# An attention and mixture kernel on one core: the first two pairs by TensorE instead of transfers, and the second expert product's first half in slices of 128 columns

## The chip, the cores and the metric

The kernel runs on one core of a Trainium2 chip. The metric is device time in microseconds (us), from the start to the end of one execution. The core has TensorE (matrix products, written to PSUM in 8 banks), DVE (VectorE), ACT (ScalarE), GpSimd (POOL) and SyncE (SP), which only issues transfers here. Transfers run on 16 DMA engines. The engines work through their own queues in program order and wait for one another by semaphores.

## The reference

Attention with a decay bias, then a soft mixture of experts over its output:

```python
cum = np.cumsum(np.maximum(s, 0.0), axis=-1)
bias = -(cum[:, :, :, None] - cum[:, :, None, :])
scores = np.where(causal, -1e9, scale * q @ k.T + np.minimum(bias, 0.0))
attn = softmax(scores) @ v                     # 8 batches x 8 heads, 576 x 64
logits = x @ phi                               # x: 4608 x 512, 32 slots
slot_input = softmax(logits, axis 0).T @ x     # 8 experts x 4 slots
slot_out[e] = np.maximum(slot_input[e] @ w1[e], 0.0) @ w2[e]
out = softmax(logits, axis 1) @ slot_out       # 4608 x 512
```

All arrays are fp32. Each expert has w1 of 512 x 1024 and w2 of 1024 x 512.

## The kernel before

**Pairs.** The 64 heads are worked on in 32 pairs of heads; a pair's q and k lie transposed on 128 partitions, 64 for each head. For pair p the steps are these. `load.p` fetches q and k, `cast.p.i` (ACT, line 341) rounds q (i=0) or k (i=1) to the matmul's short form fp32r, and `low.p.i` (DVE, line 347) subtracts that from the original to keep the low part. `mx.p.g` (TensorE, lines 375 to 379) are four groups of products for the row maxima: q times k, plus ones times the running sums of s. `red.p.g.a` (DVE, lines 381 to 392) reduces them. `f0` (GpSimd, lines 403 and 404) splits the maxima in a high and a low part, `f1` (line 411) turns them by one TensorE transpose, `f2` (ACT, line 417) copies them out of PSUM, and `md` (lines 422 to 427) sends them by a transfer into rows of the tile `g`, four rows out of 128 spread to every 32nd partition and the next one. `cum.p` (lines 355 to 360) sends the running sums' high and low parts into `g` as well. `s.p.g` (lines 438 to 446) are the scores: three short-form products of high and low parts and one of `g`, which adds sums and maxima. `ex` (ACT) is the exponential, `cut` (GpSimd) sets what is above the diagonal to zero, `z` (GpSimd) and `sm` (TensorE) add up the rows, `ax` and `a` (TensorE, lines 522 and 533) multiply by v in full fp32. fp32 products show as two instructions each, fp32r products as one.

**Sums.** Ahead of the pairs `s` is loaded to 64 partitions (line 238), clamped (DVE, line 267), summed by a scan (line 268), and split into `cumhl`, high (line 271) and low (line 272), both on DVE. The pairs 0 to 3 take their sums from `cumhl`; `cw` (line 875) copies it to DRAM for the others.

**Order.** The whole program is written out in one order, the string ORDER, made by a planner; each engine and the SP queue take their steps in that order. A step `busy.n` is n fp32 products of the identity that nothing uses (line 937): filler for TensorE. Of the 46 in the head, 28 stand ahead of the first maxima, 9 behind mx.1.0, and 3 and 6 on either side of mx.2.0 and mx.1.2. SP, which issues most transfers, waits in its queue for whatever the next transfer needs: `load.p` needs the low parts of pair p-2, since there are two buffers.

**The end.** After the last pair come the mixture's products: `mlp1` (line 995), `turn` (line 1012), then `mlp2(half, eg)` (lines 1017 to 1030), for each half of 256 of the 512 output columns and each group of four experts 8 steps; `steps(m, n)` runs n of them. `pick(half)` (line 1035) adds up the experts' rows, and `part(b, n, half)` (lines 1055 to 1067) makes the outputs of n batches for that half by four row tiles of 32 partitions, copies them out on ACT and DVE and sends them, 512 rows a batch of 1 KB each. `heads` (line 1070) sends the first 64 rows of each batch. In the kernel before, the first half's products are finished, then the second half's steps are interleaved with the first half's parts. Weights are fetched up to the second product, through the same SP queue as the outputs.

Of the kernel before, what the change touches and what calls it, by code (L numbers as in the profile page):

```python
# [24 lines left out]
load.0 load.1 cast.0.1 cast.0.0 cast.1.1 low.0.1 cum.0 cast.1.0 low.0.0 cum.1 low.1.1 low.1.0 load.3 busy.28 mx.0.0  # L25
mx.0.1 cum.2 red.0.0.1 mx.0.2 red.0.0.0 load.2 red.0.1.1 mx.0.3 red.0.1.0 red.0.2.0 mx.1.0 red.0.3.0 red.0.3.1
red.0.2.1 red.1.0.1 busy.9 mx.1.1 f0.0 red.1.0.0 cast.2.0 mx.1.3 red.1.1.0 f1.0 red.1.1.1 f2.0 cast.2.1 red.1.3.0 md.0
busy.3 mx.2.0 low.2.0 mx.1.2 red.1.3.1 load_v.0 red.2.0.0 red.1.2.1 cw red.2.0.1 busy.6 s.0.0 red.1.2.0 s.0.2 f0.1
ex.0.0.1 ex.0.0.0 s.0.1 ex.0.2.1 cut.0.0 s.0.3 ex.0.2.0 ex.0.1.0 cut.0.2 mx.2.3 ex.0.1.1 zc.0 f1.1 red.2.3.0 a.0.0
f2.1 z.0.0 ex.0.3.0 md.1 red.2.3.1 cast.3.1 ax.0 a.0.1 ex.0.3.1 evx.0 load_v.1 mx.2.2 cut.0.3 mx.2.1 cut.0.1 red.2.2.0  # L30
z.0.1 cum.3 a.0.2 a.0.3 red.2.2.1 a.0.4 s.1.0 ev.0 z.0.2 red.2.1.1 cast.3.0 red.2.1.0 s.1.2 ex.1.0.0 z.0.3 low.3.1
f0.2 ex.1.0.1 s.1.1 ex.1.2.0 low.2.1 mx.3.0 ex.1.1.0 sm.0 red.3.0.1 load.4 cut.1.0 ex.1.2.1 red.3.0.0 load_v.2 f1.2
ex.1.1.1 cut.1.2 s.1.3 zc.1 f2.2 z.1.0 mx.3.3 md.2 ex.1.3.1 mx.3.2 ex.1.3.0 red.3.3.1 a.1.0 red.3.3.0 cum.4 cut.1.1
a.1.1 red.3.2.0 cut.1.3 z.1.1 cast.4.1 ax.1 a.1.2 red.3.2.1 cast.4.0 a.1.3 a.1.4 evx.1 low.3.0 mx.3.1 z.1.2 s.2.0
red.3.1.1 load.5 red.3.1.0 s.2.2 ex.2.0.1 z.1.3 ex.2.0.0 f0.3 s.2.1 ex.2.2.0 mx.4.0 ex.2.2.1 cut.2.0 f1.3 ex.2.1.0
red.4.0.0 sm.1 f2.3 low.4.0 ex.2.1.1 md.3 mx.4.3 zc.2 cut.2.1 red.4.0.1 ev.1 cut.2.2 mx.4.2 red.4.3.1 z.2.0 s.2.3
red.4.3.0 a.2.0 ex.2.3.1 cum.5 red.4.2.0 ex.2.3.0 cast.5.1 pre.0 a.2.1 cut.2.3 load_v.3 low.4.1 z.2.1 a.2.2 red.4.2.1
a.2.3 ax.2 a.2.4 evx.2 mx.4.1 load_v.4 ev.2 s.3.0 z.2.2 red.4.1.0 cast.5.0 red.4.1.1 cst s.3.2 low.5.0 z.2.3 ex.3.0.0
load.6 ex.3.0.1 s.3.1 ex.3.2.0 f0.4 mx.5.0 ex.3.1.0 sm.2 cut.3.0 red.5.0.0 ex.3.2.1 red.5.0.1 f1.4 ex.3.1.1 cut.3.2
low.5.1 s.3.3 zc.3 f2.4 z.3.0 mx.5.3 md.4 ex.3.3.1 mx.5.2 ex.3.3.0 red.5.3.0 mx.5.1 red.5.2.0 a.3.0 pre.1 load.7  # L40
cut.3.3 cum.6 red.5.3.1 a.3.1 cut.3.1 z.3.1 pre.2 red.5.1.1 a.3.2 red.5.2.1 ax.3 a.3.3 evx.3 cast.6.0 a.3.4 z.3.2
red.5.1.0 s.4.0 load_v.5 ev.3 low.6.0 f0.5 cast.6.1 s.4.2 ex.4.0.1 low.6.1 ex.4.0.0 s.4.1 z.3.3 ex.4.2.0 pre.3 cut.4.0
mx.6.0 ex.4.2.1 load.8 sm.3 red.6.0.0 ex.4.1.0 cut.4.2 phi ex.4.1.1 f1.5 e1.0.0.0 s.4.3 f2.5 cut.4.1 zc.4 md.5
red.6.0.1 mx.6.3 z.4.0 ex.4.3.0 mx.6.2 ex.4.3.1 red.6.3.0 cast.7.1 mx.6.1 cum.7 red.6.3.1 cast.7.0 ax.4 a.4.0 rw.0.0
evx.4 cut.4.3 red.6.2.0 z.4.1 a.4.1 red.6.2.1 a.4.2 pre.4 a.4.3 red.6.1.0 z.4.2 a.4.4 red.6.1.1 s.5.0 ev.4 load_v.6
low.7.0 f0.6 s.5.2 low.7.1 rd.0 ex.5.0.0 ex.5.0.1 s.5.1 z.4.3 ex.5.2.0 cut.5.0 rd.1 mx.7.0 ex.5.2.1 sm.4 ex.5.1.0
red.7.0.0 cut.5.2 ex.5.1.1 red.7.0.1 f1.6 load.9 s.5.3 f2.6 cut.5.1 zc.5 md.6 mx.7.3 z.5.0 ex.5.3.0 mx.7.2 ex.5.3.1
cast.8.1 mx.7.1 cum.8 cast.8.0 a.5.0 nr.0 cut.5.3 a.5.1 red.7.3.0 rd.2 z.5.1 a.5.2 red.7.3.1 a.5.3 nr.1 a.5.4 z.5.2
red.7.2.0 pre.5 s.6.0 rd.3 red.7.2.1 z.5.3 nat.0 ex.6.0.0 red.7.1.0 nat.1 natd.0 red.7.1.1 sm.5 natd.1 low.8.0 f0.7
ex.6.0.1 s.6.2 nr.2 low.8.1 s.6.1 cut.6.0 ex.6.2.0 ex.6.2.1 load.10 mx.8.0 ex.6.1.0 f1.7 nat.2 red.8.0.0 cut.6.2  # L50
ex.6.1.1 red.8.0.1 natd.2 s.6.3 cut.6.1 nr.3 f2.7 zc.6 mx.8.3 md.7 ex.6.3.0 z.6.0 mx.8.2 ex.6.3.1 red.8.3.0 cast.9.1
mx.8.1 red.8.3.1 cum.9 cast.9.0 lt.0 lt.1 red.8.2.0 pre.6 lt.2 cut.6.3 lt.3 z.6.1 red.8.2.1 nat.3 c0.0 c1.0 natd.3
red.8.1.0 nat0.0 red.8.1.1 z.6.2 ax.5 natd0.0 s0.0 s.7.0 load_v.7 evx.5 f0.8 ev.5 low.9.0 s1.0 s.7.2 ex.7.0.0 z.6.3
s2.0 ex.7.0.1 s.7.1 t2.0 s2p.0 ex.7.2.0 cut.7.0 mx.9.0 ex.7.2.1 sm.6 ex.7.1.0 red.9.0.0 cut.7.2 ex.7.1.1 red.9.0.1
f1.8 low.9.1 s.7.3 f2.8 cut.7.1 zc.7 md.8 t3.0 mx.9.3 z.7.0 mx.9.2 red.9.3.0 ex.7.3.0 cum.10 ex.7.3.1 t5.0 cast.10.1
red.9.3.1 mx.9.1 load.11 cast.10.0 a.6.0 red.9.2.0 cut.7.3 t6.0 z.7.1 a.6.1 red.9.2.1 a.6.2 red.9.1.0 z.7.2 a.6.3
red.9.1.1 a.6.4 ax.6 low.10.0 ax.7 evx.6 load_v.8 f0.9 s.8.0 evx.7 ev.6 t4.0 low.10.1 s.8.2 pre.7 ex.8.0.0 z.7.3
load.12 ex.8.0.1 s.8.1 ex.8.2.0 cut.8.0 mx.10.0 ex.8.2.1 sm.7 ex.8.1.0 red.10.0.0 cut.8.2 ex.8.1.1 t7.0 e1.1.0.0 zc.8
cut.8.1 z.8.0 red.10.0.1 rw.1.0 f1.9 t8.0 s.8.3 f2.9 md.9 mx.10.3 ex.8.3.0 mx.10.2 ex.8.3.1 red.10.3.0 cast.11.1
cut.8.3 mx.10.1 cum.11 red.10.3.1 cast.11.0 z.8.1 a.7.0 rd.4 red.10.2.0 a.7.1 rd.5 z.8.2 red.10.2.1 a.7.2 a.7.3  # L60
red.10.1.0 z.8.3 a.7.4 ax.8 red.10.1.1 ev.7 load_v.9 s.9.0 low.11.0 evx.8 f0.10 s.9.2 low.11.1 pre.8 ex.9.0.0 ex.9.0.1
s.9.1 load.13 nr.4 ex.9.2.0 cut.9.0 mx.11.0 ex.9.2.1 rd.6 sm.8 ex.9.1.0 red.11.0.0 cut.9.2 ex.9.1.1 red.11.0.1 f1.10
nat.4 nr.5 f2.10 cut.9.1 zc.9 md.10 s.9.3 natd.4 z.9.0 mx.11.3 ex.9.3.0 mx.11.2 ex.9.3.1 rd.7 red.11.3.0 cast.12.1
mx.11.1 red.11.3.1 cast.12.0 nat.5 cut.9.3 cum.12 red.11.2.0 a.8.0 natd.5 z.9.1 a.8.1 red.11.2.1 pre.9 a.8.2 z.9.2
red.11.1.0 a.8.3 red.11.1.1 a.8.4 z.9.3 low.12.0 ev.8 load_v.10 s.10.0 f0.11 nr.6 s.10.2 ex.10.0.0 ex.10.0.1 s.10.1
nr.7 ex.10.2.0 cut.10.0 low.12.1 mx.12.0 ex.10.2.1 lt.4 ex.10.1.0 red.12.0.0 cut.10.2 load.14 lt.5 ex.10.1.1
red.12.0.1 lt.6 cut.10.1 lt.7 sm.9 c0.1 f1.11 t2.1 c1.1 zc.10 nat.6 f2.11 s0.1 z.10.0 md.11 nat.7 natd.6 nat0.1 natd.7
s.10.3 s1.1 natd0.1 s2.1 mx.12.3 ex.10.3.0 cum.13 mx.12.2 ex.10.3.1 s2p.1 red.12.3.0 cast.13.1 pre.10 mx.12.1 cut.10.3
red.12.3.1 cast.13.0 a.9.0 z.10.1 t3.1 red.12.2.0 a.9.1 red.12.2.1 z.10.2 a.9.2 a.9.3 red.12.1.0 a.9.4 z.10.3 ax.9
ax.10 red.12.1.1 evx.9 load_v.11 s.11.0 evx.10 ev.9 low.13.0 f0.12 t4.1 s.11.2 low.13.1 ex.11.0.0 ex.11.0.1 s.11.1  # L70
load.15 ex.11.2.0 cut.11.0 mx.13.0 ex.11.2.1 sm.10 ex.11.1.0 red.13.0.0 cut.11.2 ex.11.1.1 red.13.0.1 f1.12 t5.1 f2.12
cut.11.1 zc.11 s.11.3 md.12 t6.1 z.11.0 mx.13.3 ex.11.3.0 mx.13.2 ex.11.3.1 red.13.3.0 cum.14 cast.14.1 mx.13.1
red.13.3.1 cast.14.0 a.10.0 pre.11 cut.11.3 red.13.2.0 z.11.1 a.10.1 red.13.2.1 a.10.2 a.10.3 z.11.2 red.13.1.0 a.10.4
ax.11 red.13.1.1 ev.10 load_v.12 s.12.0 low.14.0 z.11.3 evx.11 s.12.2 low.14.1 ex.12.0.0 f0.13 ex.12.0.1 s.12.1
ex.12.2.0 load.16 mx.14.0 ex.12.2.1 cut.12.0 sm.11 ex.12.1.0 red.14.0.0 ex.12.1.1 t7.1 cut.12.2 e1.2.0.0 zc.12
cut.12.1 z.12.0 red.14.0.1 rw.2.0 f1.13 t8.1 s.12.3 f2.13 md.13 mx.14.3 ex.12.3.0 mx.14.2 ex.12.3.1 red.14.3.0
cast.15.1 cut.12.3 mx.14.1 cum.15 red.14.3.1 cast.15.0 z.12.1 a.11.0 rd.8 red.14.2.0 a.11.1 rd.9 z.12.2 red.14.2.1
a.11.2 a.11.3 red.14.1.0 z.12.3 a.11.4 ax.12 pre.12 red.14.1.1 ev.11 s.13.0 load_v.13 low.15.0 evx.12 f0.14 s.13.2
low.15.1 ex.13.0.0 ex.13.0.1 s.13.1 load.17 nr.8 ex.13.2.0 cut.13.0 mx.15.0 ex.13.2.1 rd.10 sm.12 ex.13.1.0 red.15.0.0
# [1101 lines left out]
```

## Time and profile before

| what | us |
|---|---|
| median of 3 runs | 415.88 |
| lowest and highest | 414.98 and 417.01 |
| the profiled execution's own time | 415.59 |
| its span, first to last instruction | 413.9 |
| TensorE busy | 395.3 (96%) |
| DVE, ACT, GpSimd busy | 284.0, 239.6, 274.8 |

Times of the trace count from the start of the span. Time of the execution less its span, 1.69 us, lies around the span. A line such as L445 is a line of the kernel before.

### The profile page before, as it was taken

Reading aid. Unit: us, or ns where it says so; the run is one execution under the profiler, and the core shown is the slowest. Engines: PE = TensorE matmul, PEld = TensorE weight load, DVE = VectorE, ACT = ScalarE, POOL = GpSimd, SP = SyncE. Lnnn points to the kernel's source line nnn. Section 1 sums busy time; section 2 is a strip of 40 time slices with the busy share of each in tenths; the row PEclk is TensorE's granted clock in tenths of the full one; section 3 lists DMA queues with packets and bytes.
Section 4 is the critical chain, followed back from the end, with each engine's and each line's share of the span. In section 5 each row is a group of like instructions: output and inputs, shape, how many; then the busy total and the mean of one; then the engine's idle time right before and its main releaser. Section 6 shows DMA issues by size and latency. Waiting matters only on the chain.

```text
span 413.9 us, 14533 instructions
## 1 busy us (share of the span) xinstructions
PE 395.3 (96%) x5699; PEld 295.3 (71%) x5699; DVE 284.0 (69%) x952; ACT 239.6 (58%) x717; POOL 274.8 (66%) x376
## 2 busy tenths in 40 slices
...
GB/s 130 133 80 140 181 260 261 171 89 202 231 172 144 146 232 172 141 148 216 188 142 144 229 176 144 146 193 110 92 89 191 250 234 401 390 412 384 306 329 295
DMA packets 35252, 83.76 MB, mean 202 GB/s; under 512 B 4976, under 2 KB 14192, under 8 KB 35184
## 3 DMA queue, kind: packets, MB, share of 16 engines
...
## 4 chain that ended last, share of the span: by engine, by line
PE 81%; DMA 4%; DVE 3%; ACT 2%; issue 2%; SPq 0%; DVEq 0%
PE s L445 25%; PE y L533 19%; PE mx L378 11%; PE sum L562 4%; PE m L1023 3%; PE m L995 3%; DMA g<-hl 3%; PE nat L601 3%; PE lt L666 2%; PE sl L786 2%; PE mt L411 1%; PE po L1061 1%; ACT arena L456 1%; PE x L522 1%; DVE arena L392 1%
## 5 line engine op out<-in xcount | busy, mean ns | idle before, releaser
L456 ACT ACTIVATE arena<-s 128x288 f32<-128x288 f32 (+4 forms) x384 | 114.9, 407 | 31.7 <-PE s L445 30.6
L445 PE MATMUL s<-w 64*128 64x288 f32 (+4 forms) x1152 | 109.2, 304 | 0.3 <-DVE nmin L743 0.2
L533 PE MATMUL y<-arena 128*64 128x512 f32 (+4 forms) x640 | 90.8, 427 | 0.0
L445 PEld LDWEIGHTS s<-w 64*128 64x128 f32 (+1 forms) x1152 | 81.9, 177 | 10.2 <-ACT arena L456 1.2
L463 POOL TENSOR_SCALAR_AFFINE_SELECT arena<-arena 128x256 f32<-128x256 f32 (+1 forms) x160 | 63.7, 411 | 23.6 <-ACT arena L456 22.0
L484 POOL TENSOR_TENSOR arena<-arena 128x896 f32<-128x896 f32 x31 | 69.3, 2237 | 8.7 <-PE mt L411 5.9
L533 PEld LDWEIGHTS y<-arena 128*64 128x64 f32 x640 | 42.5, 137 | 44.8 <-issue 34.1
L392 DVE CUSTOM_DVE_ANT_0 arena<-mx,arena 128x448 bf16<-128x448 f32 (+3 forms) x128 | 59.0, 461 | 17.6 <-PE mx L378 15.8
L378 PE MATMUL mx<-w 64*128 64x288 f32 (+4 forms) x384 | 56.6, 302 | 0.9 <-ACT w L341 0.9
L445 PE MATMUL s<-g 64*128 64x288 f32 (+4 forms) x384 | 56.5, 291 | 0.5 <-DMA g<-hl 0.5
L392 DVE CUSTOM_DVE_ANT_0 junk<-mx,arena 64x64 bf16<-64x64 f32 (+3 forms) x128 | 49.2, 385 | 10.4 <-PE mx L378 8.7
L378 PE MATMUL mx<-g,ones 64*128 64x288 f32 (+4 forms) x384 | 53.1, 300 | 0.0
L347 DVE TENSOR_TENSOR w<-arena,w 128x576 fp32r<-128x576 f32 x64 | 50.6, 810 | 0.2
L486 POOL TENSOR_TENSOR arena<-arena 128x640 f32<-128x640 f32 x31 | 48.3, 1557 | 2.4
L341 ACT CAST w<-arena 128x576 fp32r<-128x576 f32 x64 | 40.4, 677 | 13.7 <-DMA arena<-in_qk_dram 12.7
L545 ACT COPY arena<-y 128x512 f32<-128x512 f32 x32 | 18.8, 589 | 48.8 <-PE y L533 48.8
L389 DVE TENSOR_REDUCE mx<-mx 128x1 f32<-128x288 f32 x64 | 26.7, 447 | 27.5 <-PE mx L378 23.3
L378 PEld LDWEIGHTS mx<-w 64*128 64x128 f32 x384 | 38.5, 185 | 3.2 <-ACT w L341 1.0
L378 PEld LDWEIGHTS mx<-g,ones 64*128 64x128 f32 x384 | 38.2, 185 | 0.3
L445 PEld LDWEIGHTS s<-g 64*128 64x128 f32 (+1 forms) x384 | 35.1, 177 | 1.5 <-DMA g<-hl 1.0
L488 POOL TENSOR_TENSOR arena<-arena 128x384 f32<-128x384 f32 x31 | 31.8, 1026 | 2.4
L403 POOL TENSOR_SCALAR mh<-mx 128x10 fp32r<-128x10 f32 x32 | 20.1, 627 | 17.5 <-DVE mx L392 17.1
...
## 6 DMA issues: line engine op xcount, KB each, us to landing
...
```

The source lines that it names most:

```text
L341: nc.scalar.copy(w[:, o:o + S], st["raw", p][:, i, :])
L347: nc.vector.tensor_tensor(w[:, o + 2 * S:o + 3 * S], st["raw", p][:, i, :], w[:, o:o + S].bitcast(F32), op=ALU.subtract)
L378: nc.tensor.matmul(ps[a][:, d:d + hi - lo], l[r], t[r, k + lo:k + hi], start=t is w, stop=t is gt)
L389: nc.vector.tensor_reduce(m[:, a, c:c + 1], ps[:, d:d + w], axis=AX.X, op=ALU.max)
L392: nc.vector.tensor_tensor_reduce(out=junk()[r, 0:w], in0=ps[r, d:d + w], in1=mask[r, o:o + w], scale=1.0, scalar=m[:, a, 4:5] if i == 1 el ...
L445: nc.tensor.matmul(ps[a][0:n, d:d + hi - lo], t[r, ko + 128 * j:ko + 128 * j + n], t[r, qo + lo:qo + hi], start=x == 0, stop=x == 3)
L456: nc.scalar.activation(st["p", p][0:n, a, o + lo:o + hi], ps[0:n, d:d + hi - lo], AF.Exp, bias=0.0, scale=0.125)
L463: nc.gpsimd.affine_select(d, d, pattern=[[0, 2], [1, n]], compare_op=ALU.is_ge, fill=0.0, base=0, channel_multiplier=-1)
L484: eng.tensor_tensor(z[:, :, 128:576], pt[:, :, 128:576], pt[:, :, 576:1024], op=ALU.add)
L486: eng.tensor_tensor(z[:, :, 256:576], z[:, :, 256:576], pt[:, :, 1024:1344], op=ALU.add)
L488: eng.tensor_tensor(z[:, :, 384:576], z[:, :, 384:576], pt[:, :, 1344:1536], op=ALU.add)
L533: nc.tensor.matmul(y[r, lo - 64:512], vt[:, j, r], st["p", p][:, g, OFF[j] + lo - 128 * j:OFF[j] + 576 - 128 * j], start=(j == 0), stop=(j ...
```

## The change

**Sums.** `s` comes with even and odd heads apart and is loaded as two halves, to partitions 0 to 31 by SP and 64 to 95 by the ACT queue; two DVE memsets clear the other partitions, ahead of DVE's other set-up. Clamp and scan stay. The split into high and low becomes two ordered steps, `ch.0` on ACT and `ch.1` on GpSimd. `cum.0` and `cum.1` wait for `ch.1`.

**Maxima.** For the pairs 0 and 1 the sums' term of `mx` no longer reads `g`: a column of the identity, repeated 128 times, selects the pair's row out of the scan's result in full fp32, so `mx` waits for the scan and not for `cum`. `f0` runs on DVE and writes into a tile `turn`, which GpSimd's set-up clears and in which ones stand; `f1` is 20 fp32 products of `turn` with the identity into two banks, which gives the rows of `g` in place; `f2` and `md` are ACT copies of 512 and 128 columns into `g`. `low.0` and `low.1` move from DVE to GpSimd.

**The order.** All four fillers of the head go and one of 12 comes. The head, before and after (the middle differs in the order of neighbouring steps up to pair 8, and phi, cst and some pre fetches move):

```
load.0 load.1 cast.0.1 cast.0.0 cast.1.1 low.0.1 cum.0 cast.1.0 low.0.0 cum.1 low.1.1 low.1.0 load.3 busy.28 mx.0.0
mx.0.1 cum.2 red.0.0.1 mx.0.2 red.0.0.0 load.2 ... mx.1.0 ... busy.9 mx.1.1 f0.0 ... mx.1.3 ... md.0
busy.3 mx.2.0 low.2.0 mx.1.2 red.1.3.1 load_v.0 red.2.0.0 red.1.2.1 cw red.2.0.1 busy.6 s.0.0

load.0 load.1 cast.0.1 cast.0.0 ch.0 busy.12 mx.0.0 cast.1.1 mx.0.1 cast.1.0 red.0.0.0 red.0.0.1 mx.0.2 red.0.1.1
red.0.1.0 mx.0.3 red.0.2.0 ch.1 red.0.2.1 mx.1.0 low.0.0 red.0.3.0 cum.0 mx.1.2 cum.1 red.0.3.1 f0.0 low.0.1 red.1.0.0
f1.0 red.1.2.0 low.1.1 load.2 red.1.0.1 f2.0 load_v.0 red.1.2.1 mx.1.1 md.0 low.1.0 s.0.0 red.1.1.1 red.1.1.0 s.0.3
ex.0.0.0 load.3 mx.1.3 ex.0.0.1 cum.2 ex.0.3.0 phi cut.0.0 ex.0.3.1 s.0.1 cw cast.2.0 red.1.3.0 cut.0.3 cast.2.1 s.0.2
red.1.3.1 ex.0.1.0 f0.1 ax.0 low.2.1 ex.0.2.0 cum.3 f1.1 evx.0 ex.0.1.1 low.2.0 ex.0.2.1 cut.0.1 zc.0 mx.2.0 load.4
cut.0.2 cast.3.0 mx.2.3 red.2.0.1 z.0.0 f2.1 red.2.0.0 a.0.0 red.2.3.1 md.1 red.2.3.0 mx.2.1 s.1.0
```

**The end.** The first half of `mlp2` becomes two quarters of 128 columns. The parts of batches 0 to 3 come by quarters, four batches at a time, with 512 B to a row; those of batches 4 to 7 as halves, two at a time.

```diff
+    hb = ar["u", NP % NU]
+    s_sb = arena[:, hb:hb + S]
+    ones_s = arena[:, hb + S:hb + 2 * S]
+    cum = arena[:, hb + 2 * S:hb + 3 * S]
+    nc.vector.memset(s_sb[NP:64], 0.0)
+    nc.vector.memset(s_sb[64 + NP:128], 0.0)
+    nc.sync.dma_start(out=s_sb[0:NP], in_=s[0:NP])
+    nc.scalar.dma_start(out=s_sb[64:64 + NP], in_=s[NP:NH])
...
-    nc.vector.tensor_copy(cumhl[:, 0, :].bitcast(F32R), cum)
-    nc.vector.tensor_tensor(cumhl[:, 1, :].bitcast(F32R), cum, cumhl[:, 0, :], op=ALU.subtract)
...
+    turn = arena[:, x0:x0 + 128 * NCH].rearrange("p (c k j) -> p c k j", c=NCH, j=32)
+    nc.gpsimd.memset(turn, 0.0)
+    nc.gpsimd.memset(turn[:, :, :, 0], 1.0)
...
+    op(("ch", 0), lambda: nc.scalar.copy(cumhl[:, 0, :].bitcast(F32R), cum))
+    op(("ch", 1), lambda: nc.gpsimd.tensor_tensor(cumhl[:, 1, :].bitcast(F32R), cum, cumhl[:, 0, :], op=ALU.subtract), [("ch", 0)])
...
-            nc.vector.tensor_tensor(w[:, o + 2 * S:o + 3 * S], st["raw", p][:, i, :],
+            (nc.gpsimd if p < 2 else nc.vector).tensor_tensor(w[:, o + 2 * S:o + 3 * S], st["raw", p][:, i, :],
...
-                for l, t, k in ((w[:, q0 - 128:q0], w, WK), (ones2, gt, KO)):
+                for l, t, k in ((w[:, q0 - 128:q0], w, WK), (ones2, gt, KO) if p > 1 else (None, cum, 0)):
                     for a, r in enumerate(half):
+                        x = ident[r, 64 * a + p:64 * a + p + 1].broadcast_to([64, 128]) if l is None else l[r]
...
         def f0():
+            if p < 2:
+                mh = [turn.rearrange("p c (a l) j -> p a l c j", a=2)[:, :, l, :, 1] for l in range(2)]
+                nc.vector.tensor_scalar(mh[0].bitcast(F32R), m, 1.0, None, op0=ALU.mult)
+                nc.vector.tensor_tensor(mh[1].bitcast(F32R), m, mh[0], op=ALU.subtract)
+                return
...
         def f1():
+            if p < 2:
+                st["mt", p] = [bank(f"mt{i}") for i in range(2)]
+                for c in range(NCH):
+                    for k in range(4):
+                        nc.tensor.matmul(st["mt", p][c // 4][32 * k:32 * k + 32, 128 * (c % 4):128 * (c % 4) + 128],
+                                         turn[:, c, k, :], ident, start=True, stop=True)
+                return
...
+                nc.scalar.copy(gt[:, 0:512], st["mt", p][0])
...
+                nc.scalar.copy(gt[:, 512:KO], st["mt", p][1][:, 0:KO - 512])
...
+    m = chain(mlp2(0, QT, 0), mlp2(0, QT, 1))
     steps(m, 5)
     turn(1)
     steps(m)
+    m = chain(mlp2(QT, QT, 0), mlp2(QT, QT, 1))
+    steps(m, 3)
+    pick(0, QT)
+    steps(m, 2)
+    part(0, 4, 0, QT)
+    steps(m)
+    m = chain(mlp2(HC, HC, 0), mlp2(HC, HC, 1))
+    steps(m, 2)
+    pick(QT, QT)
     steps(m, 1)
+    part(0, 4, QT, QT)
+    steps(m, 3)
+    ct(B - 1, B)
+    part(4, 2, 0, HC)
+    steps(m, 4)
+    part(6, 2, 0, HC)
+    steps(m)
+    pick(HC, HC)
```

## Rows read from the trace of the kernel before

**Rows 1.** Busy time by stage: us, PE, PEld, DVE, ACT, POOL, PEclk, DMA share, GB/s

```profile
21.22:60.00 38.78, 38.78 (x557) 30.15 (x556) 28.23 (x103) 25.64 (x80) 33.65 (x49) 1.00 0.46 150
...
90.00:320.00 230.00, 229.45 (x3449) 176.31 (x3449) 175.64 (x619) 155.78 (x482) 192.49 (x251) 1.00 0.53 164
...
356.00:380.00 24.00, 23.80 (x283) 10.06 (x281) 4.24 (x10) 2.87 (x5) 0.45 (x1) 1.00 1.02 403
```

**Rows 2.** Busy time of two single microseconds at the end, same columns

```profile
382.00:383.00 1.00, 1.00 (x24) 0.54 (x20) 0.66 (x2) 0.70 (x2) 0.00 (x0) 1.00 0.40 160
383.00:384.00 1.00, 1.00 (x24) 0.40 (x14) 0.63 (x2) 0.37 (x1) 0.00 (x0) 1.00 0.23 94
```

**Rows 3.** Timeline to 11 us: start, us, engine, line, what [idle before <-releaser]

```profile
0.79 0.61 SPq L238 DMA_DIRECT2D arena<-in_s_dram  x1
...
1.07 1.15 DVE L251 MEMSET g<- 128x576 f32 x2
...
3.75 0.64 DVE L267 TENSOR_SCALAR arena<-arena 64x576 f32<-64x576 f32 x1 [0.28 <-DMA arena<-in_s_dram]
4.50 1.67 DVE L268 TENSOR_TENSOR_SCAN arena<-arena 64x576 f32<-64x576 f32 x1
5.38 1.25 ACT L341 CAST w<-arena 128x576 fp32r<-128x576 f32 x2 [3.31 <-DMA arena<-in_qk_dram]
...
8.31 0.53 POOL L288 MEMSET acc<- 128x512 f32 x1
...
10.64 0.40 PE L378 MATMUL mx<-w 64*128 64x288 f32 x2
```

**Rows 4.** Timeline from 11 us to the first scores

```profile
11.25 0.82 DVE L389 TENSOR_REDUCE mx<-mx 128x1 f32<-128x288 f32 x2 [0.56 <-PE mx L378]
...
16.15 0.25 POOL L403 TENSOR_SCALAR mh<-mx 128x10 fp32r<-128x10 f32 x1 [7.31 <-DVE mx L392]
...
21.22 0.68 PE L445 MATMUL s<-w 64*128 64x288 f32 x6
```

**Rows 5.** Busy time while only the first fillers run, columns as in rows 1

```profile
1.41:4.00 2.59, 2.59 (x12) 2.59 (x13) 1.88 (x11) 0.66 (x1) 2.31 (x5) 1.00 0.63 171
```

**Rows 6.** Chain of waits, TensorE pieces: start, us, engine, tile, line

```profile
32.71 0.64 PE sum L562 x32
...
93.67 2.74 PE y L533 x20
...
102.42 1.41 PE mx L378 x20
...
381.20 1.08 PE po L1061 x16
```

**Rows 7.** Costliest groups: ACT's copies of 512 columns out of PSUM

```profile
L545 ACT COPY arena<-y 128x512 f32<-128x512 f32 x32 | 18.8, 589 | 48.8 <-PE y L533 48.8
```

**Rows 8.** Costliest groups: GpSimd's two-input steps (busy us, mean ns of one)

```profile
L486 POOL TENSOR_TENSOR arena<-arena 128x640 f32<-128x640 f32 x31 | 48.3, 1557 | 2.4
...
L488 POOL TENSOR_TENSOR arena<-arena 128x384 f32<-128x384 f32 x31 | 31.8, 1026 | 2.4
```

**Rows 9.** Chain of waits at 152 us: a transfer of maxima on a loaded queue

```profile
152.00 6.41 DMA g<-hl
```

**Rows 10.** Timeline of the end: the first outputs, the second half's first part

```profile
383.09 15.54 SPq L1067 DMA_DIRECT2D out_dram<-pre  x20
...
393.64 1.15 PE L1061 MATMUL po<-pre,e_nat 32*128 32x256 f32 x16 [0.44 <-ACT pre L1036]
```

**Rows 11.** DMA queues, 345 to 380 us and 384 to 394 us: packets, MB, share

```profile
q1 hardware_dynamic: 3970, 14.06, 101.6%
...
q1 hardware_dynamic: 3275, 3.18, 93.8%
```

**Rows 12.** Timeline near 31 us: DVE's low steps beside GpSimd's split (f0)

```profile
30.94 1.62 DVE L347 TENSOR_TENSOR w<-arena,w 128x576 fp32r<-128x576 f32 x2
...
31.25 0.75 POOL L403 TENSOR_SCALAR mh<-mx 128x10 fp32r<-128x10 f32 x1
```

361 lines of the change are left out of this document (172 added, 189 removed).

## The prediction, made before the changed kernel was run

> **What bounds the kernel now.** I read the busy time by stage first, then the order of instructions at both ends. TensorE is busy for 38.78 of the 38.78 us from 21.22 to 60 and for 229.45 of the 230 us from 90 to 320 [rows 1]. So the end is set by the work queued on TensorE, and time can only be won where TensorE does no needed work: ahead of its first maxima, up to its first scores, and at the end, where the outputs leave. There another limit rules: the DMA share is 1.02 from 356 to 380 [rows 1], and once the weights are in there is a hole, 0.40 and 0.23 in the two microseconds from 382 to 384 [rows 2].
>
> At the start, fillers cover waits. The first maxima run at 10.64, though the first casts began at 5.38 and the scan, begun at 4.50, took 1.67 [rows 3]: the time between goes to the high and low parts of the sums and their transfer. The first maxima are split on GpSimd (f0) from 16.15, and the first scores start at 21.22 [rows 4]: a product, a copy and a transfer lie between.
>
> **The head, part by part.** All times are those of the profiled execution (span 413.9, time 415.59; the median of the runs, 415.88, lies 0.29 above).
>
> *Sums.* Two more DVE memsets of 576 columns (two took 1.15) now stand ahead of the clamp, which idled 0.28 for s until 3.75; DVE reaches it near 4.5 instead. Clamp 0.64 and scan 1.67 then end near 6.95 [rows 3]. The halves of s are smaller than the one transfer, so I leave 3.75 for their landing; if the ACT queue's half is 0.8 later than 4.5, all below moves by that. The cast and subtraction of the sums leave DVE, and the first mx waits for neither them nor the transfer: it starts near 7.0, 3.6 earlier. The remaining filler is 24 instructions of 0.216 us (12 in 2.59, the granted clock reading 1.00, 2.4 GHz) and ends at 6.6 [rows 5]; that cover is just enough.
>
> *Maxima in full fp32.* Pairs 0 and 1 each stream 288+288+512+512 = 1600 columns of sums against an fp32 selector. The trace has no such product on half the rows. The nearest are fp32 products of four row tiles, two rounds of 256 columns in 1.08 us, 2.1 ns a column, and of two column tiles, 1536 columns in 2.74, 1.8 ns [rows 6]. If the two halves run side by side, a pair costs 1600 x 1.8 to 2.1 = 2.9 to 3.4, in place of about 0.86 in the present form (1312 columns of two terms in 1.41, [rows 6]). I take 3.0, since the columns are long: +2.1 a pair; one after the other would be +5.1. But DVE sets the pace: its eight reductions ran from 11.25 to the split at 16.15, 4.8 us [rows 4]. First result near 7.8, last reduction near 12.7, the two steps of the split, now on DVE, to 13.0 (an estimate, below the 0.25 that GpSimd took for one).
>
> *Rows by TensorE instead of transfer.* f1 becomes 20 fp32 products of 128 columns, four column tiles side by side: 5 rounds. The same form with 72 columns took 0.64 for four rounds, 0.16 a round [rows 6], so 0.16 x 72 to 128 columns gives at most 0.28; I take 0.23, 1.15 in all. Then two ACT copies: 0.59 for 512 columns [rows 7], a quarter of that and its fixed part, 0.26, for 128. The rows stand near 14.9.
>
> *What becomes late next: GpSimd and the sums' transfer.* GpSimd's last set-up step ended at 8.84 (8.31 + 0.53) [rows 3]; that set-up waits for DVE's memsets, now 1.05 later, and gains a 640-column memset (0.6) and a small one: free near 10.6. A two-input step of 576 columns, which the trace lacks, lies on the line from 384 columns at 1026 ns to 640 at 1557: 1.43 [rows 8]. In its order come ch.1 (to 12.1), low.0.0 (13.5), low.0.1 (14.9), low.1.1, low.1.0 (17.8). Scores still need cum.0: ch.1 at 12.1, two issues of 0.5, and a flight. Its bounds: s, 144 KB, landed 2.35 after its issue ended [rows 3]; on a loaded queue 6.4 lie between an ACT copy and the scores [rows 9]. Traffic is low here, so 2.2: landed at 15.4. Three paths (14.9, 14.9, 15.4) meet; first scores near 15.4, 5.8 earlier.
>
> *What TensorE still owes.* Before, all of mx.1 and mx.2.0 were done by then; now mx.1.3 (1.15) and mx.2.0 (0.27) come after, and f1.1 adds 1.15: 2.6. One wait is new. On SP, load.2 stands behind cum.0 and cum.1 and waits for the lows of pair 0; load_v.0, load.3 (waits for low.1.0, 17.8) and cum.2 stand behind it. cum.2 is issued near 18.5 behind 576 KB and lands near 22, while mx.2.0 could run at 21.2: 0.8 lost. On ACT the casts of pair 3 stand ahead of f2.1 and md.1: load.3 issued at 18.0, 4.0 to its cast (load.0, issued at 1.4 behind s, was cast at 5.38, [rows 3]), then 0.67 + 0.59 + 0.26: 23.5, in time for s.1.0 near 24. Head: 5.8 - 2.6 - 0.8, and some 0.6 back for the old transpose and the gaps in the old stretch: **-3.0**, from -4.5 (no wait, short flight) to 0. From there the work per pair is as before; GpSimd is next fullest, 33.65 of 38.78 us [rows 1], and does not slow it. The second copy of cw and the earlier phi, cst and pre fetches cost SP issues of about 0.5 that nothing waits for; if that cover goes, load.4 and load.5 are late by as much.
>
> **The tail.** Slices of 128 columns: 16 steps of 0.23 (two rounds of at most 0.12 each) make 3.7 a quarter, 7.4 for what took 6.9, and one more pick 0.5: the second half's product ends 1.0 later. The first output left at 383.09 [rows 10]; the first quarter's are ready near 379.5, but the weights hold the DMA engines to 382.4 [rows 2], so they start then and the hole of 1.4 us closes. Packets fall from 1 KB to 512 B in 2.1 MB. Rows give 143 ns for 3.54 KB (3970 packets, 101.6% of 16 engines x 35 us) and 45.8 ns for 971 B (3275, 93.8% of 16 x 10) [rows 11]. The line through both is 9.1 ns + 0.0378 ns a byte, 28.4 ns for 512 B: 4096 packets over 16 engines take 7.3 us in place of 5.9. The ends are 22.9 ns (in proportion) and 45.8 (no gain from being short). So the first half's writes run from 382.4 to 395.8; before, they left from 383.8 and took 12.2 (343 GB/s by the line), to 396 at the least and, with gaps of some 0.9 between parts, to 396.9. The second half's first part ran at 393.64 [rows 10], its outputs near 395.5; they come near 396.4 now, and 5.24 MB need 15.3 us: 411.7 against 412.2 or so, **-0.6**, ends -1.5 and +3.2.
>
> The Trainium skill, "DMA: Bandwidth & Descriptors", Specifications, states line rate from 512 B up; by it the tail would be -1.0. The rows speak against it: packets of 971 B moved 21 B a ns and engine where 3.54 KB moved 25 [rows 11].
>
> Sum: -3.0 - 0.6 = -3.6. Span 410.3, profiled time 412.0, median **412.3**.
>
> **Rivals.** *GpSimd's low parts are stretched (slower).* Beside DVE's low step, two SBUF operands, GpSimd's split took 0.75; alone 0.25 [rows 4, 12]. At 2.9 us for each of the five steps low.1.0 ends at 25.1, load.3 is cast at 29.3, s.1.0 follows near 30.8 instead of 24: head +3.8, total +3.2, 419.1. All gain is gone from 2.2 us a step on. Against it: the reductions beside them read one operand from PSUM. [...]
>
> *A transfer is still on the way.* The sums' rows still travel before the scores (cum.0). With a flight of 4.4 scores start at 17.6: 414.5. For it, the loaded flight [rows 9]; against it, idle queues. A TensorE still slow at 7.0 would cost as much.
>
> *512 B packets cost 45.8 ns:* first-half writes end at 400.1, tail +3.2, 416.1.
>
> *The fp32 halves run one after the other:* 3.0 more a pair, of which DVE's pace hides 1.3 in pair 0: +4.7, 417.0.
>
> *Everything fits:* -4.5 and -1.5, 409.9.
>
> **Numbers.** Forecast with the full fit 0.66; transfer on the way 0.11; short packets 0.07; serial halves 0.05; stretched GpSimd, or another chain through load.2 and load.3, 0.11. A measurement of this kernel tells about 0.5% (2.1 us). Faster by more, below 413.8: 0.67, the forecast and a little of the transfer's case; within: 0.21; slower, above 418.0: 0.12. The range goes from the full fit, 409.9, to the short packets, 416.1.
>
> **What would show it.** Right: mx.0.0 near 7, f0.0 near 13, s.0.0 near 15.4, s.1.0 near 24, then the old pace; no hole in the DMA share near 380. Wrong: GpSimd steps of 576 columns well above 1.5 us, s.0.0 after 17.5 behind a transfer, ACT's waits for load.2 or load.3 reaching TensorE, fp32 mx groups above 1.2 us, packets of 512 B near 46 ns.

## The result, and the profile of the changed kernel

The changed kernel takes **421.18 us** (median of 4 runs, 419.26 to 422.68) against 416.44 for the kernel before beside it (414.98 to 417.16): a ratio of 1.0126, interval 1.0094 to 1.0158. By the ratio it is slower by 5.2 us (the two medians differ by 4.7) where 3.6 less was forecast, and outside the range. The page of the profiled execution (422.68 us) begins:

```profile
span 421.0 us, 14935 instructions
...
PE 397.0 (94%) x5895; PEld 297.2 (71%) x5895; DVE 288.1 (68%) x954; ACT 241.7 (57%) x721; POOL 281.0 (67%) x379
```

TensorE still fills the span, so the time went into gaps and into slow stretches of that engine. The table by stage of the changed kernel shows where (window, length, then busy us of PE, PEld, DVE, ACT, POOL, PEclk, DMA share, GB/s, as in [rows 1]):

```profile
14.00:15.00 1.00, 0.11 (x5) 0.03 (x5) 1.00 (x2) 0.00 (x0) 1.00 (x2) 0.99 0.04 9
15.00:16.00 1.00, 1.00 (x20) 0.93 (x24) 0.97 (x4) 0.00 (x0) 1.00 (x1) 0.50 0.13 18
16.00:17.00 1.00, 1.00 (x26) 0.80 (x18) 0.94 (x4) 0.00 (x0) 1.00 (x2) 0.50 0.94 226
...
50.00:60.00 10.00, 9.47 (x123) 6.71 (x121) 8.77 (x25) 5.33 (x17) 7.85 (x9) 1.00 0.44 148
...
80.00:90.00 10.00, 8.33 (x145) 6.96 (x147) 8.31 (x27) 5.09 (x15) 8.00 (x12) 0.83 1.00 359
...
392.00:394.00 2.00, 2.00 (x33) 1.15 (x29) 0.52 (x2) 0.58 (x2) 0.00 (x0) 1.00 0.33 94
```

The same view of the kernel before, for the two stretches that were to stay as they were:

```profile
50.00:60.00 10.00, 10.00 (x171) 7.76 (x167) 8.02 (x26) 6.75 (x22) 9.44 (x16) 1.00 0.77 244
...
80.00:90.00 10.00, 9.70 (x161) 8.10 (x160) 7.76 (x31) 8.21 (x26) 9.18 (x14) 1.00 0.49 149
```

Three places lose: the head (idle in the microsecond from 14, then 1.2 GHz), 50 to 60 us (0.53 idle), and 80 to 90 us (1.37 more idle than before, and the half clock again: the mean of three microseconds from 87 is 0.50). The end is the fourth: the DMA share falls to 0.33 at 392 to 394, where the hole of [rows 2] was to be closed. One stretch goes the other way: from 70 to 80 us TensorE is busy 9.37 of the 10 us before and 10.00 now.

The timeline of the changed kernel's head, which answers to [rows 3, 4]:

```profile
6.49 0.40 PE L387 MATMUL mx<-w 64*128 64x288 f32 x2 [0.56 <-ACT w L349]
...
10.77 1.41 POOL L324 TENSOR_TENSOR arena<-arena 128x576 fp32r<-128x576 f32 x1
12.13 5.49 POOL L355 TENSOR_TENSOR w<-arena,w 128x576 fp32r<-128x576 f32 x4
...
13.20 0.36 DVE L413 TENSOR_SCALAR arena<-mx 128x10 fp32r<-128x10 f32 x1
13.59 1.32 DVE L414 TENSOR_TENSOR arena<-mx,arena 128x10 fp32r<-128x10 f32 x1
...
14.97 2.36 PE L427 MATMUL mt<-ident,arena 128*32 128x128 f32 x38 [0.89 <-DVE arena L414]
...
18.21 0.86 PE L466 MATMUL s<-w 64*128 64x288 f32 x6
...
23.10 0.18 DVE L414 TENSOR_TENSOR arena<-mx,arena 128x10 fp32r<-128x10 f32 x1
23.18 1.45 PE L427 MATMUL mt<-ident,arena 128*32 128x128 f32 x40
...
26.89 0.56 PE L466 MATMUL s<-w 64*128 64x288 f32 x6
```

Read the two L414 rows against each other. It is one step on 10 columns. At pair 1, with GpSimd idle, it takes 0.18. At pair 0 it takes 1.32 and ends at 14.91, where GpSimd's second low part ends (12.13 + 2 x 1.37 = 14.87). TensorE stands behind it for 0.89, and has just stood 0.49 for the step before, and after that the granted clock is 0.50: the first scores come at 18.21, not 15.4. Those of pair 1 follow at 26.89, where 24 was expected: the delay of some 2.8 stays.

To compare kernels of different order I use one mark: the start of ACT's copy of y of pair 8, by when all of them have done nearly the same work (117 us, past all three losses):

| kernel | mark, us | against before | median, us | ratio, interval |
|---|---|---|---|---|
| before | 116.64 | | 415.4 to 416.4 | |
| after | 120.44 | +3.80 | 421.18 | 1.0126 [1.0094, 1.0158] |
| e3_f0_gpsimd | 118.13 | +1.49 | 418.95 | 1.0076 [1.0052, 1.0101] |
| e6_f0_gpsimd_old_end | 118.39 | +1.75 | 417.81 | 1.0042 [1.0017, 1.0068] |
| e5_head_then_old_order | 115.65 | -0.99 | 414.22 | 0.9963 [0.9937, 0.9989] |
| e9_low_moved | 117.33 | +0.69 | 415.90 | 1.0015 [0.9998, 1.0033] |
| e12_low_and_nr_moved | 114.98 | -1.66 | 415.32 | 0.9989 [0.9960, 1.0017] |

The mark comes from one profile of each kernel. Four pairs of kernels whose code is the same up to it show how well it repeats: 120.44 and 120.52 (after, e1), 118.13 and 118.39 (e3, e6), 116.64 and 117.81 (before, e2), 118.80 and 116.62 (e10, e11). A difference of one or two us at the mark can therefore be chance. The mark helps to find where a profile lost time; what an edit is worth is told by the runs. Behind the mark some profiles have a further stall of about 1 us (1.05 at 199 us in the changed kernel) that others lack.

### The profile page after: what moved, and what is told of

Read it like the earlier page. It is cut to its first block, busy times and chain, and to the rows that moved or that the text cites. A ratio compares the mean times of both kernels' runs of the same rounds, so it can differ in the third digit from the quotient of the medians.

```text
span 421.0 us, 14935 instructions
## 1 busy us (share of the span) xinstructions
PE 397.0 (94%) x5895; PEld 297.2 (71%) x5895; DVE 288.1 (68%) x954; ACT 241.7 (57%) x721; POOL 281.0 (67%) x379
## 4 chain that ended last, share of the span: by engine, by line
PE 80%; DVE 6%; DMA 5%; issue 3%; POOL 1%; SPq 1%; ACT 0%; DVEq 0%
PE s L466 23%; PE y L554 18%; PE mx L387 11%; PE sum L583 4%; PE m L1048 4%; PE m L1019 3%; DMA arena<-rs 3%; PE nat L622 3%; PE lt L687 2%; PE sl L807 2%; PE po L1086 1%; PE mt L432 1%; DVE arena L401 1%; DVE arena L614 1%; PE nat L699 1%
## 5 line engine op out<-in xcount | busy, mean ns | idle before, releaser
L484 POOL TENSOR_SCALAR_AFFINE_SELECT arena<-arena 128x256 f32<-128x256 f32 (+1 forms) x160 | 66.1, 427 | 29.1 <-ACT arena L477 27.5
L505 POOL TENSOR_TENSOR arena<-arena 128x896 f32<-128x896 f32 x31 | 67.9, 2192 | 7.7 <-PE mt L432 5.5
L401 DVE CUSTOM_DVE_ANT_0 arena<-mx,arena 128x320 bf16<-128x320 f32 (+3 forms) x128 | 59.3, 464 | 15.2 <-PE mx L387 13.6
L387 PE MATMUL mx<-w 64*128 64x288 f32 (+4 forms) x384 | 58.7, 313 | 0.6 <-ACT w L349 0.6
L401 DVE CUSTOM_DVE_ANT_0 junk<-mx,arena 128x192 bf16<-128x192 f32 (+3 forms) x128 | 48.7, 381 | 8.4 <-PE mx L387 6.6
L355 DVE TENSOR_TENSOR w<-arena,w 128x576 fp32r<-128x576 f32 x60 | 49.4, 839 | 0.9 <-POOL mh L418 0.8
L387 PE MATMUL mx<-g,ones 64*128 64x288 f32 (+1 forms) x360 | 48.7, 299 | 0.0
L387 PEld LDWEIGHTS mx<-w 64*128 64x128 f32 x384 | 37.4, 186 | 4.4 <-ACT g L447 0.8
L387 PEld LDWEIGHTS mx<-g,ones 64*128 64x128 f32 x360 | 34.8, 186 | 0.3
L614 DVE TENSOR_TENSOR arena<-arena 128x576 f32<-128x576 f32 x30 | 28.2, 953 | 1.4 <-DMA arena<-rs 1.4
```

Source lines behind the costliest of these rows:

```text
L355: (nc.gpsimd if p < 2 else nc.vector).tensor_tensor(w[:, o + 2 * S:o + 3 * S], st["raw", p][:, i, :], w[:, o:o + S].bitcast(F32), op=ALU.s ...
L387: nc.tensor.matmul(ps[a][:, d:d + hi - lo], x, t[r, k + lo:k + hi], start=t is w, stop=t is not w)
L401: nc.vector.tensor_tensor_reduce(out=junk()[r, 0:w], in0=ps[r, d:d + w], in1=mask[r, o:o + w], scale=1.0, scalar=m[:, a, 4:5] if i == 1 el ...
L484: nc.gpsimd.affine_select(d, d, pattern=[[0, 2], [1, n]], compare_op=ALU.is_ge, fill=0.0, base=0, channel_multiplier=-1)
L505: eng.tensor_tensor(z[:, :, 128:576], pt[:, :, 128:576], pt[:, :, 576:1024], op=ALU.add)
L614: nc.vector.tensor_tensor(u, u, st.pop(("r", p)), op=ALU.mult)
```

## The experiments: the end

**e1_old_end**: the changed kernel with `mlp2`, `pick`, `part` and their calls as in the kernel before.

```diff
-    m = chain(mlp2(0, QT, 0), mlp2(0, QT, 1))
+    m = chain(mlp2(0, 0), mlp2(0, 1))
...
-    part(0, 4, 0, QT)
+        part(b, 2, 0)
```

> The changed kernel with the end of the kernel before (second product by halves); its head and order stay. If the slices cost time because the second half's product ends later (the trace of the changed kernel has its first part 2.6 us later after mlp1 than before), 2 to 2.5 us come back: 419. If the slices close the hole in the DMA share as forecast, taking them away costs 0.6: 421.8.

Measured: 418.92 (418.27 to 420.68), ratio 1.0062 [1.0037, 1.0086]. **e2_new_end** is the reverse, the kernel before with the new end alone.

> The kernel before with only the new end. First theory (TensorE feeds the outputs too late): 2 to 2.5 us slower than before, 418.6, with the DMA share well under 1 for some 4 us after the first outputs. Rival (the forecast): 0.6 faster, 415.8.

Measured: 417.89 (415.79 to 419.20), ratio 1.0028 [1.0005, 1.0050]. So the new end costs some 2 by itself (1.8 and 2.3 by the medians, 1.2 and 2.7 by the ratios), where 0.6 less was forecast. The rest, some 3 us, belongs to the other part of the change.

The chain of waits of the changed kernel's end (start, us, what) shows what the end waits for:

```profile
378.32 3.19 PE m L1048 x112
381.51 0.42 PE sel L1060 x2
...
382.50 1.10 PE po L1086 x32
383.61 0.34 PE m L1048 x2
383.94 0.87 issue
384.81 3.46 PE m L1048 x101
...
389.27 0.66 PE po L1086 x16
389.92 0.25 issue
390.18 0.73 PE po L1086 x16
...
401.17 1.18 PE po L1086 x16
```

The slices run as costed: 112 matmuls, 28 rounds, in 3.19, 0.114 a round. But from the first product step to the second half's first part TensorE takes 25.15 (376.02 to 401.17) where it took 22.57 (371.07 to 393.64, [rows 10]): 2.6 more. Of that 1.12 is "issue", time in which the engine waited for nothing that the profile shows. A stall of 0.87 to 1.07 stands in each of the four profiles with this end (after, e2, e3, e4) and in none with the old one.

The packets were not at fault. In e2, from 386.5 to 388.5 us, the queue moved (packets, MB, share of 16 engines):

```profile
q1 hardware_dynamic: 844, 0.41, 68.9%
```

That is 0.689 x 16 x 2 us / 844 = 26.1 ns for a packet of 512 B; 28.4 was taken. The Trainium skill, "DMA: Bandwidth & Descriptors", Specifications, states line rate from 512 B up; by an estimate from that and the longest packets of the rows it would be 20.7 ns (143 x 512 / 3540, [rows 11]), which the trace does not reach.

**e11_sliced_product_only** tells whether the stall goes with the slices or with the quarter parts and their early transfers. It is e10 (below, old end) with the product of the first half in two slices, and one pick and parts of 256 columns as before:

```diff
-    m = chain(mlp2(0, 0), mlp2(0, 1))
+    m = chain(mlp2(0, QT, 0), mlp2(0, QT, 1), mlp2(QT, QT, 0), mlp2(QT, QT, 1))
```

> As e10, with the first half of the second product in two slices of 128 columns, but picks, parts and transfers as in the kernel before. If TensorE's stall without a releaser (0.87 to 1.07, only with the new end) belongs to the slices' twice as dense instructions: it shows here too, and the time is 0.8 to 1.2 above e10. If it belongs to the quarter parts and their early transfers: no stall, and 0 to 0.4 above e10.

Measured: 418.16 against 416.97 of e10, 1.2 more, though with six runs the intervals of the two ratios overlap. What decides is the chain of e11:

```profile
373.40 4.71 PE m L1045 x165
378.11 1.80 issue
379.90 2.15 PE m L1045 x56
```

The stall is there without a quarter part or an early output, and longer. From the first product step to the pick e11 takes 10.79 (371.28 to 382.07), e10 8.67 (372.41 to 381.08): 2.1 more, 1.80 of it the stall. So it goes with the slices, which ask for twice as many TensorE instructions per microsecond (four matmuls each 0.11 instead of 0.215).

One row of the traces bears on the cause: a queue named "instruction". In the changed kernel it shows one packet from 382 to 383 us, and in e11 the same from 377 to 378 (packets, MB, share of 16 engines):

```profile
q8 instruction: 1, 0.02, 6.7%
```

These are blocks of 16 KB that take about 1.1 us each. The profile of the changed kernel has 46 of them for 11790 matmuls and weight loads, that of the kernel before 45 for 11398: in both, one for some 255, so I take this queue to be TensorE's. In e11 the block sets out at 377.43 and TensorE goes on at 379.90; in the changed kernel at 382.39 and 384.81. With shorter stalls that follow in three of the profiles there are eight in all, of 0.25 to 1.80, and each ends 2.4 to 2.6 us after such a block sets out. So TensorE seems to wait there for its next instructions. Full transfer queues are not needed for it: the DMA share is 1.0 in the first stall of each profile, but 0.60 in the second one of e3 (0.80, at 386.56). This is an agreement of times; no experiment moved the blocks themselves.

## The experiments: the head

**e3_f0_gpsimd**: the two split steps of pairs 0 and 1 go to GpSimd, where they stand in its order between two low parts.

```diff
-                nc.vector.tensor_scalar(mh[0].bitcast(F32R), m, 1.0, None, op0=ALU.mult)
-                nc.vector.tensor_tensor(mh[1].bitcast(F32R), m, mh[0], op=ALU.subtract)
+                nc.gpsimd.tensor_scalar(mh[0].bitcast(F32R), m, 1.0, None, op0=ALU.mult)
+                nc.gpsimd.tensor_tensor(mh[1].bitcast(F32R), m, mh[0], op=ALU.subtract)
```

> The changed kernel with f0 of the pairs 0 and 1 on GpSimd, between its low parts, instead of on DVE beside them. If DVE's two-operand step stood still for GpSimd's low part (1.32 us instead of 0.18) and TensorE's clock fell because it stood idle meanwhile, f1.0 starts near 14.0 instead of 14.97 and runs in 1.5 instead of 2.4 us, and the first scores start near 16 instead of 18.2; the time falls by 1.5 to 2.5, to 419. Rival (the later chain through the transfers of batch 0 decides): the first scores come earlier, the time stays within 0.7 of 421.2.

Measured: 418.95 (417.69 to 421.71), 2.2 below the changed kernel. Its timeline:

```profile
13.50 0.27 POOL L413 TENSOR_SCALAR arena<-mx 128x10 fp32r<-128x10 f32 x1
13.85 0.22 POOL L414 TENSOR_TENSOR arena<-mx,arena 128x10 fp32r<-128x10 f32 x1
...
15.85 0.77 PE L466 MATMUL s<-w 64*128 64x288 f32 x6
```

The granted clock reads 1.00 in every window of its head, and the first scores come at 15.85, 2.36 before the changed kernel's and 0.45 after the forecast.

**e4_fill** leaves the split on DVE and puts seven fillers ahead of f1.0, so that only the slow stretch goes and the held step stays:

```diff
-f1.0 red.1.2.0 low.1.1
+busy.7 f1.0 red.1.2.0 low.1.1
```

> The changed kernel with 7 filler products ahead of f1.0, so that TensorE does not stand idle from 13.2 to 15 us. If the fall of its clock to half from 15 to 18.4 is what that wait brought, the granted clock stays at 1.00, f1.0 takes 1.5 instead of 2.4 us, the first scores start near 16.7 instead of 18.2, and the time falls by about 1.5, to 419.7. If the clock falls whatever runs there, or if the head does not decide, the time stays at 421.

Measured: 421.10 (419.95 to 421.69), ratio 1.0107 [1.0081, 1.0134]: no gain clear of noise. In its profile the granted clock reads 1.00 throughout the head, and the timeline shows the effect there:

```profile
14.91 1.37 PE L427 MATMUL mt<-ident,arena 128*32 128x128 f32 x40
...
16.71 0.51 PE L466 MATMUL s<-w 64*128 64x288 f32 x1
17.67 0.63 PE L466 MATMUL s<-w 64*128 64x288 f32 x5 [0.45 <-DVE mx L401]
```

From f1 to the first scores 1.80 pass, where the changed kernel took 3.24 (14.97 to 18.21): the half clock cost 1.44, and of the 2.36 that e3 won, 0.92 is the held step. The scores' second bank then waits for reductions (0.45). The times do not confirm what this is worth, and do not rule it out: the intervals of the changed kernel and of e4 overlap so far that 1.5 could hide in them. What the fillers win in the whole kernel stays open.

## The experiments: the order of the later steps

**e6_f0_gpsimd_old_end** joins e1 and e3; **e5_head_then_old_order** adds to it, from f2.2 of pair 2 (30 us) on, the order of the kernel before; **e7_old_order_from_f2_5** does so from f2.5 (57 us) on.

```diff
 a.0.3 a.0.4 z.0.3 f1.2 low.3.1 mx.3.0 f2.2
-cut.1.0 s.1.2 md.2 red.3.0.0 red.3.0.1 s.1.1
+ev.0 s.1.2 s.1.1 ex.1.2.0 ex.1.1.0 sm.0 red.3.0.1
```

> The changed kernel with f0 of pairs 0 and 1 on GpSimd and the end of the kernel before, in the new order throughout. If both edits add up: 418.95 less the 2.3 that the old end was worth, 416.7, the time of the kernel before. If the old end is worth nothing once the head is earlier: 418.9. It is the measure for the other two.

> The changed kernel with three edits: f0 of pairs 0 and 1 on GpSimd, the end of the kernel before, and, from f2.2 on (about 30 us), the order of steps of the kernel before in place of the new one. Theory A (the new order of the later steps itself costs TensorE time at 51 to 60 and 80 to 94 us; the head's own gain, 1.5 us at 40 us, would be kept): 414 to 415, 1.5 below the kernel before, and TensorE busy 9.4 or more of the 10 us from 80 to 90. Theory B (the losses come with any early head, since the passes of the normalization just collide at another time): 416 to 417, as e6 beside it.

> As e6, but with the order of the kernel before from f2.5 on (about 57 us). By theory A the loss of 1.5 at 51 to 60 us stays and that of 2.8 at 80 to 94 goes: 415 to 416. If the whole loss lies in the pairs ahead of that point: 416.7, as e6. If the switch of orders itself costs: above 417.

Measured: e6 417.81, e5 **414.22** (413.58 to 417.03), e7 418.14 (416.71 to 420.17). The early head is worth something once the rest keeps its old order: 0.37% below the kernel before, and e5's copies of y of pairs 1 to 12 are all earlier by 0.97 to 1.00 than in the profile of the kernel before (by 1.25 to 2.17 than in that of e2, which has the same code there). The new order of later steps costs 3.6 (e6 less e5; 3.3 by the ratios). Theory A holds, but not the split of the loss that e7 was to show: there TensorE is busy 9.92 of the 10 us from 80, as A said, but only 9.10 of the 10 from 60, where e6 has 10.00 and e7 has a new wait of 0.70 for a pair's rows, and nothing is saved.

What the order does there is seen in the changed kernel's timeline:

```profile
53.09 2.08 POOL L505 TENSOR_TENSOR arena<-arena 128x896 f32<-128x896 f32 x1
...
53.34 2.44 DVE L355 TENSOR_TENSOR w<-arena,w 128x576 fp32r<-128x576 f32 x1
...
59.24 0.83 PE L466 MATMUL s<-w 64*128 64x448 f32 x5 [0.49 <-DVE mx L401]
...
81.88 2.11 POOL L505 TENSOR_TENSOR arena<-arena 128x896 f32<-128x896 f32 x1
83.94 0.40 POOL L484 TENSOR_SCALAR_AFFINE_SELECT arena<-arena 128x256 f32<-128x256 f32 x1
...
82.80 2.17 DVE L614 TENSOR_TENSOR arena<-arena 128x576 f32<-128x576 f32 x1 [0.79 <-DMA arena<-rs]
...
85.70 0.43 PE L687 MATMUL lt<-arena 128*32 128x128 f32 x8 [1.67 <-DVE mx L401]
```

Both times a DVE step on two SBUF operands (alone 0.75) begins while GpSimd's addition over 896 columns runs. The first ends at 55.78, 0.6 after the addition (55.17). The second ends at 84.97, 0.6 after the masking step that follows the addition at once (84.34): held out to there, it then took little less than its own time. The pair's reductions (L401) stand behind it on DVE, and TensorE waits for the PSUM banks that these free. It is the mechanism of the head once more. The kernel before has the same pair of steps at 81 us, the other way round:

```profile
80.97 0.75 DVE L593 TENSOR_TENSOR arena<-arena 128x576 f32<-128x576 f32 x1
...
81.00 2.70 POOL L484 TENSOR_TENSOR arena<-arena 128x896 f32<-128x896 f32 x1
```

DVE began 0.03 earlier, and now GpSimd took 0.6 longer (2.70 for 2.1), off the path.

**e8_pre_moved** tries a rival cause of the second loss: SP issues four weight fetches in a bunch between 77 and 84 us (DMA share 1.00 at 80 to 90), and the last normalization rows land late. It is e6 with the fetches where the kernel before has them.

```diff
-s.6.0 pre.3 red.7.1.0 pre.1 s.6.2
+s.6.0 red.7.1.0 s.6.2
```

> As e6 (417.81), with the weight fetches pre.1, pre.3, pre.4 and pre.5 put where the order of the kernel before has them, so that they no longer stand in one bunch right behind the last normalization rows (rd.3). Theory A (the loss at 80 to 94 us comes from the rows being late, which puts the last DVE step of the normalization beside GpSimd's addition over 896 columns): rows land 1 us or more earlier, that step takes near 0.75 in place of 2.18, 416.0 to 416.5. Theory B (the rows are late by themselves or the reductions are what holds TensorE): 417.8.

Measured: 417.25 against 417.81. The DMA share from 80 to 90 fell from 0.97 to 0.60, yet the rows landed no earlier (DVE waited until 81.92, in e6 until 81.87), the step took 1.87, and TensorE waited 1.44. The bunch is not the cause.

**e9_low_moved** is e6 with one DVE step moved behind the reductions of its pair:

```diff
-cut.3.3 zc.3 cum.6 low.6.0 a.3.0
+cut.3.3 zc.3 cum.6 a.3.0
...
-s.4.3 red.5.2.1 s.4.0
+s.4.3 red.5.2.1 low.6.0 s.4.0
```

> As e6 (417.81), with one DVE step, low.6.0, put behind the last reduction of pair 5 in place of between them. Theory A (this step is held beside GpSimd's addition over 896 columns, 2.44 in place of 0.76, and the reductions that free the scores' banks stand behind it): the idle 0.73 of TensorE at 57 to 58 us goes, 416 to 416.5. Theory B (TensorE idles there for another reason): 417.8. A later normalization can take part of it back, as it did between the changed kernel's two losses.

Measured: 415.90, below e6 by 1.9 in the medians and by 1.1 in the ratios (1.0015 and 1.0042, whose intervals overlap). The traces are clearer. First e6's row, then busy time from 50 to 60 us in e6 and in e9:

```profile
58.34 0.84 PE L466 MATMUL s<-w 64*128 64x448 f32 x5 [0.73 <-DVE mx L401]
...
50.00:60.00 10.00, 9.19 (x116) 6.35 (x117) 8.11 (x24) 4.96 (x16) 7.61 (x10) 1.00 0.44 149
...
50.00:60.00 10.00, 10.00 (x164) 7.64 (x155) 7.22 (x27) 6.23 (x20) 9.64 (x15) 1.00 0.48 153
```

The wait, 0.49 to 0.73, stands in all seven profiles with this step between the reductions (after, e1, e3, e4, e6, e7, e8) and in none of the four in which it was moved (e9 to e12). So that loss was the place of one step. **e10_pre_and_low** joins e8 and e9.

> e8 and e9 together: if the two losses are separate and both are the held DVE step, 417.81 less 3.3 to 3.6: 414.2 to 414.5, the time of e5, with the new order otherwise untouched. If one loss only moves into the other's place: 416 or more.

Measured: 416.97 against 415.90 of e9, with overlapping intervals: no gain. The second held step is still there (TensorE waits 1.70 at 85.20), and one more wait has come, for a pair's rows:

```profile
63.23 0.42 PE L463 MATMUL s<-g 64*128 64x320 f32 x2 [2.27 <-DMA g<-hl]
```

The earlier fetches now lie ahead of these rows, but that does not settle it: e11 has the same order and waits only 0.62 at this place, and e8, with the same fetches, not at all. Why the two edits do not add up stays open.

**e12_low_and_nr_moved** is e9 with the second held step moved as well. In e9 it began 0.32 after GpSimd's addition:

```profile
78.76 2.11 POOL L501 TENSOR_TENSOR arena<-arena 128x896 f32<-128x896 f32 x1
...
79.08 2.77 DVE L610 TENSOR_TENSOR arena<-arena 128x576 f32<-128x576 f32 x1 [0.17 <-DMA arena<-rs]
...
82.59 0.43 PE L683 MATMUL lt<-arena 128*32 128x128 f32 x8 [1.66 <-DVE mx L397]
```

```diff
-s.6.3 natd.2 nr.3 pre.4 cut.6.1
+s.6.3 natd.2 pre.4 cut.6.1
...
-mx.8.1 red.8.3.1 cast.9.0
+mx.8.1 red.8.3.1 nr.3 cast.9.0
```

> As e9 (415.9), with the last DVE step of the first normalization, nr.3, put behind the reductions red.8.3.0 and red.8.3.1 in place of ahead of them. In e9 it began 0.3 after GpSimd's addition over 896 columns and took 2.77 in place of 0.75, and TensorE waited 1.66 for the reductions behind it. Theory A (whichever of the two engines begins a step on two SBUF operands first holds the other out until its end): the reductions run at once, TensorE's wait falls from 1.66 to 0.5 or less, 414.4 to 414.9. Theory B (the rows' landing is what TensorE waits for, the step's place is not): lt.3 and the rows' transposes wait instead, 415.6 or more.

Measured: 415.32 (413.00 to 417.80). Its timeline:

```profile
81.11 0.76 DVE L610 TENSOR_TENSOR arena<-arena 128x576 f32<-128x576 f32 x1
...
81.11 2.15 POOL L503 TENSOR_TENSOR arena<-arena 128x640 f32<-128x640 f32 x1
...
83.75 0.60 PE L695 MATMUL nat<-ident,arena 128*64 128x128 f32 x4 [0.42 <-DVE mx L397]
```

The step takes 0.76, GpSimd's next addition pays (2.15 for 1.56, [rows 8]), and TensorE's longest wait there is 0.42, as theory A said. The time is between the two theories (414.4 to 414.9, and 415.6 or more). At the mark this kernel is ahead by 1.66, which is within what the mark varies, and its fastest run, 413.00, is the lowest of any kernel; but its runs scatter over 4.8 us and the intervals of its ratio hold 1 and overlap with those of e9. The cause of that scatter stays open. So the trace shows the mechanism at this place, and the times do not yet show its price. Of the versions run, e5 alone is measured faster than both kernels.

## Why the prediction was wrong, step by step

**Held: the costs of the new work alone.** The first maxima run at 6.49 (near 7.0). The fp32 halves ran side by side: pair 0's group took 3.03 (6.49 to 9.52, where pair 1's begins; 3.0). The last reduction ended at 13.01 (12.7). GpSimd was free at 10.77 (10.6) and its step of 576 columns took 1.41 and 1.37 (1.43). ACT's copies took 0.58 and 0.27 (0.59, 0.26). The sums' rows did not hold the scores.

**Mis-sized: f1.** 20 products took 1.45 at 2.4 GHz, not 1.15: 128 columns scaled almost in full from the row with 72. That is 0.3 a pair.

**Failed: "the two steps of the split, now on DVE, to 13.0 (an estimate, below the 0.25 that GpSimd took for one)".** Alone they do take 0.18 each. Beside GpSimd's low parts they took 0.36 and 1.32. The rival that was priced here had the right pair of engines and the wrong loser: it asked whether DVE stretches GpSimd, and dismissed it because the reductions read PSUM. GpSimd was not stretched; it held DVE. By the Trainium skill, "SBUF — State Buffer", Who interferes with whom, a DVE step with two SBUF inputs contends with a GpSimd step that reads SBUF, and issue order decides who blocks; the traces agree in both directions (1.32 for 0.18 at 13.6, 2.70 for 2.1 on GpSimd at 81 in the kernel before). The prediction reckoned with one direction only.

**Left out: the clock.** The sum put TensorE's idle time at nothing but its length. It was mostly idle from 13.2 to 15.0, the granted clock then read 0.50 (1.2 GHz) until past 18, and that cost another 1.44 up to the first scores (from the profile of e4). First scores: 0.45 for f1 and small gaps, 0.92 held, 1.44 slow, together 2.81, which is 18.21 less 15.4.

**Failed: "From there the work per pair is as before; GpSimd is next fullest ... and does not slow it."** The diff replaced the order of nearly all later steps too, and I read only its beginning closely. The rows that the sentence rests on also leave out 60 to 90 us, where TensorE idles 0.93 even in the kernel before (busy 9.37 of the 10 us from 70 and 9.70 of those from 80). e5 against e6 prices that at 3.3 to 3.6; e9 and e12 name the two DVE steps that came to start behind GpSimd's long additions. With the old order kept, the early head is worth 1.5 (e5, by the ratio; 0.5 to 2.6), not 3.0; with the new order mended at two places (e12) nothing clear of noise is left.

**Failed: "the second half's product ends 1.0 later" and with it -0.6.** The packets were as costed (26.1 ns), the first half left from 384.42 on with no hole in front, and still nothing was gained, because the second half's parts came 2.6 later by TensorE, not 1.0, and DMA idled between (0.33 at 392). Of the 2.6, 1.1 is stalls that no row of before could show, 0.4 the third pick, 0.3 the smaller parts (4.65 us for 4.32), and about 0.6 the last pick, which no longer has a part to hide behind: DVE's 0.49 and ACT's 0.38 now stand in the chain; 0.2 is not placed.

The rivals that were named (flight, short packets, serial halves) did not occur.
